# Neighbourhood attention on one core: all products 32 outputs wide, four side by side, and ten key rows for four query rows

## The chip, the cores and the metric

The kernel runs on one core of a Trainium2 chip. The metric is the time of one execution in device microseconds. Times are medians of several runs; the profile comes from one further execution, whose own time is given beside its span.

## The reference, cut to what matters

An image of 224 x 224 pixels with 192 channels goes through one projection to queries, keys and values. Each pixel attends to 49 neighbours: 7 x 7 pixels with a stride of 2 in both directions, shifted inwards at the borders. The weighted values go through a last projection.

```python
qkv = x @ wqkv                      # (1,224,224,192) @ (192,576)
off = jnp.arange(7) * 2
r0 = jnp.clip(jnp.arange(224) - 6, 0, 223 - 12)   # the same for columns
nidx = (r0[:, None] + off)[...] * W + (c0[:, None] + off)[...]
logits = jnp.einsum('bnc,bnkc->bnk', q, k[nidx]) * 192 ** -0.5
out = jnp.einsum('bnk,bnkc->bnc', softmax(logits), v[nidx]) @ wo
```

Because of the stride of 2, pixels of even and odd rows, and of even and odd columns, form four images of 112 x 112 that never mix.

## The kernel before, in words

**Weights folded.** The kernel never makes queries and keys. It computes A = Wq Wk^T (scaled, in `AW`), so that a logit is x_query A x_key, and W = Wv Wo (in `WP`), so that the values are already projected. x lies transposed in SBUF: `XA` and `XB` hold 128 rows each, where `XB` has 64 channels and, in its other 64 rows, marks of rows and columns that push a logit outside the window to about NEG, -1e30. A product over the channels therefore takes two passes (`pas` 0 with `XA`, 1 with `XB`), accumulated in PSUM.

**Steps and pairs.** The work goes in 14 steps n, each with a row class `rc` (even or odd rows) and 16 query rows. A step has 7 pairs of strips (m); a strip s is 16 query rows by 8 query columns, 128 queries, in both column classes `cc`. So there are 98 pairs k. For each, in this order in the code:

- `stage1` (L476): logits of two strips into the PSUM tiles `s` (`SS[0]` and `SS[1]`, 128 x 2 x 256), L501. The stationary operand is `g`, the folded queries; the moving operand is 14 key rows by 14 to 16 columns of `XA` or `XB`. The 128 queries are two halves h of 8 query rows, each with its own 14 key rows (`key_rows`, L468), so a half is a product 64 outputs wide, and the two halves lie in the two 64-column halves of the array, issued in turn. Then DVE reduces to the negative maximum `nmx` (L503).
- `stage1b`: ACT takes the exponentials into `p` (L511), over all 14 key rows.
- `stage2`: 16 transposes of `p` on PE into `pt_ps` (L521), 64 outputs wide, and a copy to `pt_sb` (L523).
- `stage3`: `pt_sb` times the values (`vd`, `vf`) into `o_ps` (L532), 64 wide, with a column of ones that gives the sum.
- `stage4`: DVE divides (L538, L552) and SP and POOL issue the writes (L558, L571).

Between these, for the next step, `w128` and `w64` hold the making of `g` and the values: `g_items` (L405: `pg` in `whole`, `pgh` in `halves`, matmuls at L425 through `both`), copied out by ACT or DVE (L335, L333) and for `pgh` onwards by POOL (L460), and `v_item` (L347: `pv`, matmuls at L345 in `v_mms`). POOL sorts x (L170) and copies `XB` (L160).

**Order.** The code's order of these calls is each engine's order; `in_order` fixes it. Every matmul is one instruction that loads weights (in the profile PEld) and one that streams (PE). All products are 64 outputs wide and come in twos, one for each half of the array.

**NEG in PSUM.** L143 writes NEG once into columns 0 and 1 of each of the 14 rows of 16 in `SS`, which the logits of most strips never write.

Of the kernel before, what the change touches and what calls it, by code (L numbers as in the profile page):

```python
# [21 lines left out]
NSLOT = 14  # L22
NSTEP = 14
NBAND = 14
RP = 48
RW = 2 * S
MM = 16
# [71 lines left out]
def kernel(  # L99
# [40 lines left out]

    SS = [ps_s.tile([128, 2, 256], F32, name=f"s{k}", tag=f"s{k}") for k in range(2)]
    for t in SS:
        nc.vector.memset(_win(t, 0, 128, 0, [[256, 2], [16, 14], [1, 2]]), NEG)  # L143

    def load_items(b):

# [184 lines left out]
    def evac(out_, in_, dve):  # L331
        if dve:
            nc.vector.tensor_copy(out=out_, in_=in_)  # L333
        else:
            nc.scalar.copy(out=out_, in_=in_)  # L335

    def v_mms(pv, at):  # L340
        for cc in range(2):
            for pas in range(2):
                for h in range(2):
                    k = 1 if pas else 2 * cc
                    nc.tensor.matmul(pv[64 * h:64 * h + 64, cc * C:(cc + 1) * C], lhsT=at(k, h), rhs=WP[(cc, pas)][:], start=(pas == 0), stop=(pas == 1))  # L345

    def v_item(rc, cb):  # L347
        def emit(dve):
            pv = ps_g.tile([128, 512], F32, name="pv", tag="pg")
            v_mms(pv, lambda k, h: XS[rc][:, k, cb, 64 * h:64 * h + 64])  # L350
            evac(_win(VF[rc], 0, 128, cb * VP, [[193, 2], [1, C]]), pv[:, 0:2 * C].rearrange("p (t c) -> p t c", c=C), dve)
        return emit

# [8 lines left out]
    def v_first(j):  # L362
        def emit(dve):
            pv = ps_g.tile([128, 512], F32, name="pv", tag="pg")
            v_mms(pv, lambda k, h: _win(XS[1], 0, 128, k * NSLOT * 128 + 128 * j + 64 * h, [[1, 64]]))
            evac(_win(VF[1], 0, 128, (7 + j) * VP, [[193, 2], [1, C]]), pv[:, 0:2 * C].rearrange("p (t c) -> p t c", c=C), dve)
        return emit

# [29 lines left out]
                runs.append([d - d0, 1, mem, pair])  # L398
        return runs

    OUT_A = (0, 64)
    OUT_B = (128, 0)
    GROUPS = ((0, 2), (2, 4), (6, 4), (10, 4))

    def g_items(rc, ti, s0, ns):  # L405
        rows = row_runs(rc, ti)
        w = 8 * ns

        def mm(pg, cc, p0, c0):

            out_ = []
            for (d0, dn, mem, pair) in col_runs(cc, 8 * s0, 8 * s0 + w):
                for (j, n, par, r) in rows:
                    o = _win(pg, p0, 64, j * w + d0, [[w, n], [1, dn]])
                    for pas in range(2):
                        X = (XA, XB)[pas][mem]
                        out_.append((o, AW[(mem, pas)][:, c0:c0 + 64], _win(X, 0, 128, _x(par, r, pair), [[RW, n], [1, dn]]), pas))
            return out_

        def both(a, b):  # L420
            for q in range(max(len(a), len(b))):
                for l_ in (a, b):
                    if q < len(l_):
                        (o, l, r, pas) = l_[q]
                        nc.tensor.matmul(o, lhsT=l, rhs=r, start=(pas == 0), stop=(pas == 1))  # L425

        def put(dst, off, pg, dve, p0=0, pn=128):

            a, m = s0, ns
            if s0 == 0:  # L430
                rr = [_runs8(rc, ti, h) for h in range(2)]
                if len(rr[0]) == len(rr[1]):
                    evac(_win(dst, p0, pn, off, [[64, 2], [8, 8], [1, 8]]), _win(pg, p0, pn, 0, [[8 * w, 2], [1, 8], [w, 8]]), dve)
                else:
                    for h in range(2):
                        for (j0, nj) in rr[h]:
                            evac(_win(dst, p0, pn, off + 64 * h + 8 * j0, [[nj, 8], [1, nj]]), _win(pg, p0, pn, (8 * h + j0) * w, [[1, 8], [w, nj]]), dve)
                a, m = 1, ns - 1
            evac(_win(dst, p0, pn, off + (a - s0) * 128, [[8, 16], [128, m], [1, 8]]), _win(pg, p0, pn, 8 * (a - s0), [[w, 16], [8, m], [1, 8]]), dve)

        def whole(cc):
            def emit(dve):
                pg = ps_g.tile([128, 512], F32, name="pg", tag="pg")
                both(mm(pg, cc, 0, OUT_A[cc]), mm(pg, cc, 64, OUT_A[cc] + 64))
                put(G[rc][cc], s0 * 128, pg, dve)
            return emit

        def halves(dve, direct=False):
            pg = ps_g.tile([128, 512], F32, name="pgh", tag="pg")
            pg1 = ps_o.tile([128, 512], F32, name="pgh", tag="o") if direct else pg  # L450
            both(mm(pg, 0, XDAT[0], OUT_B[0]), mm(pg1, 1, XDAT[1], OUT_B[1]))
            if direct:
                put(G[rc][0], (NSLOT + s0) * 128, pg, False, XDAT[0], 64)
                put(G[rc][1], (NSLOT + s0) * 128, pg1, True, XDAT[1], 64)
                return
            gx = work.tile([128, 512], BF, name="gx", tag="gx", bufs=3)
            put(gx, 0, pg, dve)
            for cc in range(2):
                p = XDAT[cc]
                nc.gpsimd.tensor_copy(out=G[rc][cc][p:p + 64, 1, s0:s0 + ns, :], in_=gx[p:p + 64, 0:ns * 128].rearrange("p (s q) -> p s q", q=128))  # L460

        return [whole(0), whole(1), halves]
# [2 lines left out]
    class Pair:  # L465
        pass

    def key_rows(J, h):  # L468

        i = 2 * J.ti + h  # L470
        if J.rc == 0:
            if i == 0:
                return [(MM - 6, 0, 6), (0, 6, 8)]
            v0 = 8 * i - 6
        else:
            v0 = 8 * i  # L476
        return [(v, v - v0, n) for (v, n) in _wraps(v0, 14)]

    def stage1(J, ab):
        s = 2 * J.m + ab  # L480
        s_ps = SS[ab]


        cols = {0: [(1, 7, S - 7), (8, 8, 0)], 2: [(1, 15, 9)]}.get(s, [(2, 14, 8 * s - 6)])
        lo = cols[0][0]
        for cc in range(2):
            units = []
            for h in range(2):
                u = []
                for (v, k0, n) in key_rows(J, h):  # L490
                    for (q, nq, c) in cols:
                        o = _win(s_ps, 64 * h, 64, cc * 256 + 16 * k0 + q, [[16, n], [1, nq]])
                        for pas in range(2):
                            X = (XA, XB)[pas][cc]
                            u.append((o, G[J.rc][cc][:, pas, s, 64 * h:64 * h + 64], _win(X, 0, 128, _x(J.rc, v, c), [[RW, n], [1, nq]]), pas))
                units.append(u)
            for q in range(max(len(u) for u in units)):
                for u in units:
                    if q < len(u):
                        (o, w, r, pas) = u[q]  # L500
                        nc.tensor.matmul(o, lhsT=w, rhs=r, start=(pas == 0), stop=(pas == 1))  # L501
        nmx = stat.tile([128, 2], F32, name="nmx", tag="nmx")
        nc.vector.tensor_reduce(out=nmx[:], in_=_win(s_ps, 0, 128, lo, [[256, 2], [16, 14], [1, 16 - lo]]), axis=AX.XY, op=ALU.max, negate=True)  # L503
        J.p = PP[J.rc][J.k % 2]
        J.s[ab] = (s_ps, nmx)
# [8 lines left out]
    def stage2(J):  # L514
        pool_ = ps_t if J.k < NP - 1 else ps_g
        pt_ps = pool_.tile([128, 8, 128], BF, name="pt_ps", tag="pt" if J.k < NP - 1 else "pg")
        for ab in range(2):
            for cc in range(2):
                for q in range(2):
                    for h in range(2):  # L520
                        nc.tensor.transpose(pt_ps[64 * h:64 * h + 64, 4 * ab + 2 * cc + q, :], J.p[:, ab, cc, q, 64 * h:64 * h + 64], ident[:])  # L521
        J.pt = work.tile([128, 8, 128], BF, name="pt_sb", tag="pt_sb")
        (nc.scalar.copy if J.n == NSTEP - 1 and J.m < 5 else nc.vector.tensor_copy)(out=J.pt[:], in_=pt_ps[:])  # L523

    def stage3(J, ab):
        rc, s = J.rc, 2 * J.m + ab
        o_ps = (ps_o if J.k < NP - 1 else ps_g).tile([128, 512], F32, name="o_ps", tag="o" if J.k < NP - 1 else "pg")
        V = (VD[rc], VF[rc])
        for cc in range(2):
            for q in range(2):  # L530
                for h in range(2):
                    nc.tensor.matmul(o_ps[64 * h:64 * h + 64, cc * 193:cc * 193 + 193], lhsT=J.pt[:, 4 * ab + 2 * cc + q, 64 * h:64 * h + 64],  # L532
                                     rhs=V[h][:, (s - 1 + q) % NSLOT, cc * C:cc * C + 193], start=(q == 0), stop=(q == 1))
        J.o_ps[ab] = o_ps

    def stage4a(J, ab):
# [73 lines left out]
        v_first(j)(False)  # L610

    t = ps_t.tile([128, 8, 128], BF, name="pt_ps", tag="pt")
    for q in range(16):
        nc.tensor.transpose(t[64 * (q % 2):64 * (q % 2) + 64, q // 2 % 8, :], ident[:, 64 * (q % 2):64 * (q % 2) + 64], ident[:])
    sort1 = sort_items(1, 0, dve)
    for it in xb_items(1, dve) + sort1[2:] + sort1[:2]:
        it()
# [140 lines left out]
```

## Time and profile before

| | |
|---|---|
| time, median of 3 runs (lowest to highest) | 364.49 us (363.73 to 364.56) |
| the profiled execution's own time | 362.85 us |
| its span, first to last instruction | 361.1 us |
| granted TensorE clock, mean | 0.996 |
| matmuls / weight loads on PE | 8,104 / 8,104 |
| matmuls by line: pv L345, g L425, s L501, pt_ps L521, o_ps L532 | 1,624, 1,320, 1,980, 1,568, 1,568 |
| ACT's exponentials L511 | 392 of 450 ns |
| DVE's maxima L503, and scaling L552 | 196 of 564 ns, 179 of 557 ns |
| bytes moved by DMA | 60.79 MB, 168 GB/s over the span |

PE is the matmul side of TensorE and PEld its weight loads, which overlap PE. Busy time is the union of an engine's instructions; matmuls are pipelined, so one of 192 columns is shown with some 250 ns while the next starts long before it ends. "Issue" as a releaser means that an engine was idle and waited for nothing that the profile shows. Queues q1 and so on are DMA queues; a packet is one transfer on one of 16 DMA engines.

### The profile page before, as it was taken

How to read it: one execution, taken by the hardware profiler on the slowest of the kernel's cores; microseconds unless marked ns; L12 is line 12 of the kernel's file. 1: busy time of each engine (PE TensorE's matmuls, PEld its weight loads, DVE VectorE, ACT ScalarE, POOL GpSimd, SP SyncE). 2: the span in 40 equal slices, each digit the busy share in tenths (PEclk: the TensorE clock that was granted, in tenths of full speed). 3: DMA queues.
4: the chain of work that ended last, by engine and by line, in shares of the span. 5: the costliest groups of instructions: out<-in, count | busy, mean ns of one | idle time of the engine just before them, and what ended most of it. 6: DMA issues, size and time to landing. Idle time of an engine off the chain costs nothing.

```text
span 361.1 us, 19455 instructions
## 1 busy us (share of the span) xinstructions
PE 335.6 (93%) x8104; PEld 305.8 (85%) x8104; DVE 313.7 (87%) x743; ACT 307.5 (85%) x821; POOL 285.6 (79%) x456
## 2 busy tenths in 40 slices
PE   3988888998999999999999999999999999999881
PEld 1676777997999899999989999899999999999671
DVE  8967987887998998989989999898998889989992
ACT  3654767997998999989999999999989989999792
POOL 8976799999896986959969699696995878374094
PEclk9999999999999999999999999999999999999998
DMA  9999986697988979899799998988989965634432
GB/s 188 204 175 180 174 172 148 146 199 162 202 177 201 196 164 190 186 194 192 168 183 181 197 190 177 161 213 180 198 178 192 191 146 121 143 97 108 103 80 77
DMA packets 137778, 60.79 MB, mean 168 GB/s; under 512 B 88841, under 2 KB 137166, under 8 KB 137691
## 3 DMA queue, kind: packets, MB, share of 16 engines
q1 hardware_dynamic: 130133, 56.37, 78.3%
q0 software_dynamic: 5520, 1.73, 2.7%
q10 hardware_dynamic: 2038, 1.47, 2.2%
q8 instruction: 63, 1.03, 1.2%
q14 instruction: 24, 0.20, 0.2%
HBM read 0.29 MB, written 19.27 MB: 54 GB/s over the span
## 4 chain that ended last, share of the span: by engine, by line
PE 69%; POOL 10%; DVE 8%; ACT 6%; DMA 3%; issue 2%; SPq 1%; POOLq 0%; DVEq 0%; ACTq 0%
PE pv L345 16%; PE s L501 15%; PE o_ps L532 14%; PE pg L425 10%; PE pt_ps L521 9%; PE pgh L425 5%; POOL out_dram L571 4%; ACT p L511 3%; DVE xb L160 2%; POOL xs L170 2%; POOL out_dram L558 2%; DMA out_dram<-o_sb 1%; DMA vd<-vf 1%; ACT vf L335 1%; DVE nmx L503 1%
## 5 line engine op out<-in xcount | busy, mean ns | idle before, releaser
L511 ACT ACTIVATE p<-s,nmx 128x224 bf16<-128x224 f32 x392 | 149.8, 450 | 24.5 <-DVE nmx L503 22.8
L503 DVE TENSOR_REDUCE nmx<-s 128x2 f32<-128x392 f32 (+1 forms) x196 | 102.4, 564 | 19.9 <-PE s L501 19.4
L552 DVE TENSOR_TENSOR o_sb<-o_ps,rs 128x384 bf16<-128x384 f32 x179 | 99.8, 557 | 7.1 <-DMA out_dram<-o_sb 0.9
L460 POOL COPY g<-gx 64x512 bf16<-64x512 bf16 (+1 forms) x110 | 61.8, 562 | 52.9 <-ACT gx L335 47.1
L345 PE MATMUL pv<-wp,xs 128*64 128x192 bf16 x1624 | 92.7, 250 | 7.1 <-POOL xs L170 1.9
L345 PEld LDWEIGHTS <-xs 128*64 128x64 bf16 x1624 | 78.5, 111 | 20.5 <-issue 8.8
L335 ACT CAST vf<-pv 128x384 bf16<-128x384 f32 x193 | 87.6, 518 | 9.6 <-PE pv L345 5.2
L571 POOL DMA_DIRECT2D out_dram<-o_s x150 | 84.2, 568 | 1.1 <-issue 1.1
L532 PE MATMUL o_ps<-vd,pt_sb 128*64 128x193 bf16 x784 | 82.2, 246 | 2.9 <-ACT pt_sb L523 2.1
L501 PE MATMUL s<-xa,g 128*64 128x196 bf16 (+7 forms) x990 | 82.2, 233 | 1.6 <-issue 0.5
L532 PE MATMUL o_ps<-vf,pt_sb 128*64 128x193 bf16 x784 | 82.1, 246 | 0.0
L501 PE MATMUL s<-xb,g 128*64 128x196 bf16 (+7 forms) x990 | 81.8, 232 | 0.3 <-ACT g L335 0.3
L501 PEld LDWEIGHTS <-g 128*64 128x64 bf16 x1980 | 77.6, 110 | 3.6 <-issue 2.5
L532 PEld LDWEIGHTS <-pt_sb 128*64 128x64 bf16 x1568 | 71.3, 109 | 4.9 <-ACT pt_sb L523 3.2
L523 DVE COPY pt_sb<-pt_ps 128x1024 bf16<-128x1024 bf16 x93 | 63.7, 686 | 5.4 <-PE pt_ps L521 0.6
L521 PE MATMUL pt_ps<-ident,p 128*64 128x128 bf16 x1568 | 63.9, 219 | 0.0
L521 PEld LDWEIGHTS <-p 128*64 128x64 bf16 x1568 | 57.0, 110 | 5.2
L335 ACT CAST g<-pg 128x512 bf16<-128x512 f32 (+4 forms) x136 | 57.6, 471 | 2.0 <-PE pg L425 2.0
L425 PEld LDWEIGHTS <-aw 128*64 128x64 bf16 x1320 | 54.1, 110 | 4.1 <-issue 0.7
L425 PE MATMUL pg<-xb,aw 128*64 128x512 bf16 (+9 forms) x440 | 53.9, 269 | 0.6 <-DVE xb L160 0.6
L425 PE MATMUL pg<-xa,aw 128*64 128x512 bf16 (+9 forms) x440 | 52.0, 270 | 0.0
L170 POOL COPY xs<-xa 128x896 bf16<-128x896 bf16 x50 | 45.1, 928 | 1.4
(75 smaller groups left out, 282.8 us busy)
## 6 DMA issues: line engine op xcount, KB each, us to landing
vd<-vf SPq DMA_DIRECT2D x49, 336.9 KB
out_dram<-o_sb SPq DMA_DIRECT2D x156, 96.0 KB
out_dram<-o_sb SPq DMA_DIRECT2D x26, 78.0 KB
out_dram<-o_s POOLq DMA_DIRECT2D x78, 9.0 KB, 3.9
vd<-vf SPq DMA_DIRECT2D x2, 337.8 KB
vd<-vf ACTq DMA_DIRECT2D x2, 336.9 KB
xa<-in_x_dram SPq DMA_TRANSPOSE x28
out_dram<-o_s POOLq DMA_DIRECT2D x26, 15.0 KB, 3.1
```

The lines of the kernel that those rows point to most:

```text
L335: nc.scalar.copy(out=out_, in_=in_)
L345: nc.tensor.matmul(pv[64 * h:64 * h + 64, cc * C:(cc + 1) * C], lhsT=at(k, h), rhs=WP[(cc, pas)][:], start=(pas == 0), stop=(pas == 1))
L425: nc.tensor.matmul(o, lhsT=l, rhs=r, start=(pas == 0), stop=(pas == 1))
L460: nc.gpsimd.tensor_copy(out=G[rc][cc][p:p + 64, 1, s0:s0 + ns, :], in_=gx[p:p + 64, 0:ns * 128].rearrange("p (s q) -> p s q", q=128))
L501: nc.tensor.matmul(o, lhsT=w, rhs=r, start=(pas == 0), stop=(pas == 1))
L503: nc.vector.tensor_reduce(out=nmx[:], in_=_win(s_ps, 0, 128, lo, [[256, 2], [16, 14], [1, 16 - lo]]), axis=AX.XY, op=ALU.max, negate=True)
L511: nc.scalar.activation(out=J.p[:, ab, cc, :, z:z + 112].rearrange("p q (r k) -> p q r k", k=8), in_=_win(s_ps, 0, 128, cc * 256, [[8, 2], ...
L521: nc.tensor.transpose(pt_ps[64 * h:64 * h + 64, 4 * ab + 2 * cc + q, :], J.p[:, ab, cc, q, 64 * h:64 * h + 64], ident[:])
L523: (nc.scalar.copy if J.n == NSTEP - 1 and J.m < 5 else nc.vector.tensor_copy)(out=J.pt[:], in_=pt_ps[:])
L532: nc.tensor.matmul(o_ps[64 * h:64 * h + 64, cc * 193:cc * 193 + 193], lhsT=J.pt[:, 4 * ab + 2 * cc + q, 64 * h:64 * h + 64], rhs=V[h][:, ( ...
L552: nc.vector.tensor_tensor(out=o_sb[:], in0=_win(o_ps, 0, 128, 0, [[194, 2], [1, C]]), in1=rs[:].unsqueeze(2).to_broadcast([128, 2, C]), op ...
L571: pool_q.append(lambda dst=dst, p=p, m=n * nj, cc=cc: nc.gpsimd.dma_start(out=dst.rearrange("j i c -> i j c"), in_=o_sb[p:p + m, cc, :]))
```

## The change

Every product becomes 32 outputs wide. Four of them, one for each 32-column part of the array, are issued in turn where there were two of 64. That holds for `pv`, `pg`, `pgh`, `s`, `pt_ps`, `o_ps` and the first transposes of the identity. PE's program in the built kernel has 16,168 matmuls and as many weight loads.

For the logits, a part g of the array now holds four query rows. Four query rows see only ten key rows, so `key_rows` gives ten (from row 0 or 4 of the half's fourteen), and the matmul has 10 x 14 columns. The other four key rows of that part keep what stood in PSUM: NEG, which L143 now writes to all 14 x 16 places of both column classes. Strips 0 and 2 of every step, the half with the first eight query rows of the even class and the one with the last eight of the odd class, and the first pair of step 1 still take all fourteen rows. The reduction, the exponentials, the copies and all transfers stay as they are.

```diff
-        nc.vector.memset(_win(t, 0, 128, 0, [[256, 2], [16, 14], [1, 2]]), NEG)
+        nc.vector.memset(_win(t, 0, 128, 0, [[256, 2], [1, 224]]), NEG)
...
+    def side_by_side(ls):
+        for q in range(max(len(l_) for l_ in ls)):
+            for l_ in ls:
+                if q < len(l_):
+                    (o, w, r, pas) = l_[q]
+                    nc.tensor.matmul(o, lhsT=w, rhs=r, start=(pas == 0), stop=(pas == 1))
...
-                for h in range(2):
+                for g in range(4):
                     k = 1 if pas else 2 * cc
-                    nc.tensor.matmul(pv[64 * h:64 * h + 64, cc * C:(cc + 1) * C], lhsT=at(k, h), rhs=WP[(cc, pas)][:], start=(pas == 0), stop=(pas == 1))
+                    nc.tensor.matmul(pv[32 * g:32 * g + 32, cc * C:(cc + 1) * C], lhsT=at(k, g), rhs=WP[(cc, pas)][:], start=(pas == 0), stop=(pas == 1))
...
-                both(mm(pg, cc, 0, OUT_A[cc]), mm(pg, cc, 64, OUT_A[cc] + 64))
+                side_by_side([mm(pg, cc, 32 * g, 64 * cc + 32 * g) for g in range(4)])
...
-            both(mm(pg, 0, XDAT[0], OUT_B[0]), mm(pg1, 1, XDAT[1], OUT_B[1]))
+            side_by_side([mm((pg, pg1)[cc], cc, XDAT[cc] + g, OUT_B[cc] + g) for cc in range(2) for g in (0, 32)])
...
-    def key_rows(J, h):
-        i = 2 * J.ti + h
-        if J.rc == 0:
-            if i == 0:
-                return [(MM - 6, 0, 6), (0, 6, 8)]
-            v0 = 8 * i - 6
-        else:
-            v0 = 8 * i
-        return [(v, v - v0, n) for (v, n) in _wraps(v0, 14)]
+    def key_rows(J, g, full):
+        i, k0 = 2 * J.ti + g // 2, 0 if full else 4 * (g % 2)
+        v0, n = 8 * i - (6 if J.rc == 0 else 0) + k0, 14 if full else 10
+        if v0 < 0:
+            return [(v0 + MM, k0, -v0), (0, k0 - v0, n + v0)]
+        return [(v, k0 + v - v0, m) for (v, m) in _wraps(v0, n)]
...
+                edge = (J.ti, J.rc, g // 2) in ((0, 0, 0), (NSTEP // 2 - 1, 1, 1))
+                for (v, k0, n) in key_rows(J, g, edge or s in (0, 2) or (J.n == 1 and J.m == 0)):
                     for (q, nq, c) in cols:
-                        o = _win(s_ps, 64 * h, 64, cc * 256 + 16 * k0 + q, [[16, n], [1, nq]])
+                        o = _win(s_ps, 32 * g, 32, cc * 256 + 16 * k0 + q, [[16, n], [1, nq]])
...
-                    for h in range(2):
-                        nc.tensor.transpose(pt_ps[64 * h:64 * h + 64, 4 * ab + 2 * cc + q, :], J.p[:, ab, cc, q, 64 * h:64 * h + 64], ident[:])
+                    for g in range(4):
+                        nc.tensor.transpose(pt_ps[32 * g:32 * g + 32, 4 * ab + 2 * cc + q, :], J.p[:, ab, cc, q, 32 * g:32 * g + 32], ident[:])
...
-                for h in range(2):
-                    nc.tensor.matmul(o_ps[64 * h:64 * h + 64, cc * 193:cc * 193 + 193], lhsT=J.pt[:, 4 * ab + 2 * cc + q, 64 * h:64 * h + 64],
-                                     rhs=V[h][:, (s - 1 + q) % NSLOT, cc * C:cc * C + 193], start=(q == 0), stop=(q == 1))
+                for g in range(4):
+                    nc.tensor.matmul(o_ps[32 * g:32 * g + 32, cc * 193:cc * 193 + 193], lhsT=J.pt[:, 4 * ab + 2 * cc + q, 32 * g:32 * g + 32],
+                                     rhs=V[g // 2][:, (s - 1 + q) % NSLOT, cc * C:cc * C + 193], start=(q == 0), stop=(q == 1))
```

More of the change, by code (lines that the diff above doesn't have):

```diff
@@ L349, in emit @@
             pv = ps_g.tile([128, 512], F32, name="pv", tag="pg")
-            v_mms(pv, lambda k, h: XS[rc][:, k, cb, 64 * h:64 * h + 64])
+            v_mms(pv, lambda k, g: XS[rc][:, k, cb, 32 * g:32 * g + 32])
             evac(_win(VF[rc], 0, 128, cb * VP, [[193, 2], [1, C]]), pv[:, 0:2 * C].rearrange("p (t c) -> p t c", c=C), dve)
@@ L364, in emit @@
             pv = ps_g.tile([128, 512], F32, name="pv", tag="pg")
-            v_mms(pv, lambda k, h: _win(XS[1], 0, 128, k * NSLOT * 128 + 128 * j + 64 * h, [[1, 64]]))
+            v_mms(pv, lambda k, g: _win(XS[1], 0, 128, k * NSLOT * 128 + 128 * j + 32 * g, [[1, 32]]))
             evac(_win(VF[1], 0, 128, (7 + j) * VP, [[193, 2], [1, C]]), pv[:, 0:2 * C].rearrange("p (t c) -> p t c", c=C), dve)
@@ L399, in col_runs @@
         return runs
-    OUT_A = (0, 64)
     OUT_B = (128, 0)
@@ L413, in mm @@
                 for (j, n, par, r) in rows:
-                    o = _win(pg, p0, 64, j * w + d0, [[w, n], [1, dn]])
+                    o = _win(pg, p0, 32, j * w + d0, [[w, n], [1, dn]])
                     for pas in range(2):
                         X = (XA, XB)[pas][mem]
-                        out_.append((o, AW[(mem, pas)][:, c0:c0 + 64], _win(X, 0, 128, _x(par, r, pair), [[RW, n], [1, dn]]), pas))
+                        out_.append((o, AW[(mem, pas)][:, c0:c0 + 32], _win(X, 0, 128, _x(par, r, pair), [[RW, n], [1, dn]]), pas))
             return out_
[L420 to L425, printed above, removed]
         def put(dst, off, pg, dve, p0=0, pn=128):
@@ L487, in stage1 @@
             units = []
-            for h in range(2):
+            for g in range(4):
                 u = []
-                for (v, k0, n) in key_rows(J, h):
+                edge = (J.ti, J.rc, g // 2) in ((0, 0, 0), (NSTEP // 2 - 1, 1, 1))
+                for (v, k0, n) in key_rows(J, g, edge or s in (0, 2) or (J.n == 1 and J.m == 0)):
                     for (q, nq, c) in cols:
-                        o = _win(s_ps, 64 * h, 64, cc * 256 + 16 * k0 + q, [[16, n], [1, nq]])
+                        o = _win(s_ps, 32 * g, 32, cc * 256 + 16 * k0 + q, [[16, n], [1, nq]])
                         for pas in range(2):
                             X = (XA, XB)[pas][cc]
-                            u.append((o, G[J.rc][cc][:, pas, s, 64 * h:64 * h + 64], _win(X, 0, 128, _x(J.rc, v, c), [[RW, n], [1, nq]]), pas))
+                            u.append((o, G[J.rc][cc][:, pas, s, 32 * g:32 * g + 32], _win(X, 0, 128, _x(J.rc, v, c), [[RW, n], [1, nq]]), pas))
                 units.append(u)
[L497 to L501, printed above, removed]
+            side_by_side(units)
         nmx = stat.tile([128, 2], F32, name="nmx", tag="nmx")
@@ L530, in stage3 @@
             for q in range(2):
-                for h in range(2):
-                    nc.tensor.matmul(o_ps[64 * h:64 * h + 64, cc * 193:cc * 193 + 193], lhsT=J.pt[:, 4 * ab + 2 * cc + q, 64 * h:64 * h + 64],
-                                     rhs=V[h][:, (s - 1 + q) % NSLOT, cc * C:cc * C + 193], start=(q == 0), stop=(q == 1))
+                for g in range(4):
+                    nc.tensor.matmul(o_ps[32 * g:32 * g + 32, cc * 193:cc * 193 + 193], lhsT=J.pt[:, 4 * ab + 2 * cc + q, 32 * g:32 * g + 32],
+                                     rhs=V[g // 2][:, (s - 1 + q) % NSLOT, cc * C:cc * C + 193], start=(q == 0), stop=(q == 1))
         J.o_ps[ab] = o_ps
@@ L612 @@
     t = ps_t.tile([128, 8, 128], BF, name="pt_ps", tag="pt")
-    for q in range(16):
-        nc.tensor.transpose(t[64 * (q % 2):64 * (q % 2) + 64, q // 2 % 8, :], ident[:, 64 * (q % 2):64 * (q % 2) + 64], ident[:])
+    for q in range(32):
+        nc.tensor.transpose(t[32 * (q % 4):32 * (q % 4) + 32, q // 4, :], ident[:, 32 * (q % 4):32 * (q % 4) + 32], ident[:])
     sort1 = sort_items(1, 0, dve)
```

## The prediction, as made before the change was run

> **What bounds the kernel now.** I read the page first, then stretches of time, the chain of waits in one stretch, and the one idle spot of TensorE that nothing explains. The page's busy line and two of its queue lines:
>
> ```profile
> PE 335.6 (93%) x8104; PEld 305.8 (85%) x8104; DVE 313.7 (87%) x743; ACT 307.5 (85%) x821; POOL 285.6 (79%) x456
> ...
> q1 hardware_dynamic: 130133, 56.37, 78.3%
> ...
> q8 instruction: 63, 1.03, 1.2%
> ```
>
> The reader should see three things. TensorE (PE) has the most work, with DVE and ACT not far below. The DMA engines are busy too. And queue 8 carries instructions: 63 packets of 16 KB. PE's program in the built kernel has 16,240 (8,104 matmuls, as many weight loads, a few of the sequencer's); 1.03 MB over them is 64 B each, so a packet is 256 instructions and queue 8 is PE's. So PE's program is not on the chip: it is fetched while it runs, 256 instructions at a time.
>
> The table by stretches (columns: stretch, PE, PEld, DVE, ACT, POOL busy with counts, granted clock, DMA share, GB/s):
>
> ```profile
> 215.00:240.00 25.00, 24.96 (x587) 23.06 (x583) 23.06 (x57) 23.78 (x64) 21.63 (x32) 1.00 0.99 183
> ...
> 290.00:315.00 25.00, 25.00 (x719) 24.15 (x715) 22.35 (x54) 23.24 (x69) 15.19 (x29) 1.00 0.60 133
> ```
>
> From 90 to 335 us PE has hardly an idle moment, at a granted clock of 1.00; ACT is at 92 to 95% and DVE at 88 to 92%. The chain of waits in one step of that stretch is PE alone:
>
> ```profile
> 187.16 0.66 PE pv L345 x16
> 187.82 0.69 PE s L501 x17
> 188.51 0.67 PE o_ps L532 x16
> 189.18 0.46 PE pgh L425 x4
> 189.64 0.45 PE pt_ps L521 x16
> 190.09 0.46 PE pg L425 x4
> ```
>
> Sixteen matmuls of 192 columns (pv) take 0.66 us, a pair side by side 82 ns; sixteen of 128 (pt_ps) take 0.45, a pair 56. Both are 0.43 ns a column. So PE is bound by the columns that stream through it, two products at a time. That is what the change attacks. But one view speaks of another limit close by, PE's matmuls around 155 us:
>
> ```profile
> 154.94 0.22 PE L501 MATMUL s<-xb,g 128*64 128x120 bf16 x1
> 155.61 0.28 PE L501 MATMUL s<-xa,g 128*64 128x90 bf16 x2 [0.45 <-issue]
> ```
>
> PE stands still from the start at 154.945 to the next at 155.614, released by "issue": by nothing that the profile knows. The matmul that comes late waits for no semaphore and its weights were loaded at 154.947. It is instruction 6,338 of PE's program. In the trace's packet records of queue 8 a packet had started at 153.24, only 2.37 us before PE went on. I then marked the program at instruction 194 and every 256 from there (6,338 is one of the marks). There are 63 marks and 63 packets, and 62 of the packets start between 0.03 us before and 2.43 us after PE reached a mark. The shortest time from a packet's start to the first instruction behind the next mark is 2.37 us at the stall and 2.64 us or more at all the others. The reading I choose: entering one block of 256 instructions asks for the next one, only one is on its way at a time, and a block can be used about 2.37 us after its packet starts. At the stall PE entered the block with nothing queued, and the next packet started at 157.18, 1.56 us later. **One fetch so costs 1.56 + 2.37 = 3.9 us, and PE can't be given more than 256 instructions in that time.** Before, a block lasts 5.2 us on average; the fastest two in a row took 8.1 us together. The limit was just not met.
>
> **The change part by part.**
>
> *Streams.* Counted in the built kernels, the logits (L501) stream 310,464 columns two at a time, 155,232 steps; after it is 482,048 four at a time, 120,512 steps, since most quads take 10 x 14 columns and not 14 x 14. Pairs of 196 start 84 ns apart, 0.43 ns a column: 34,720 steps less are 14.9 us of PE. The other four products (L345, L532, L521, L425) stream what they did, in quads for pairs. What falls short of this: quads of few columns. Pairs of 9 columns start 31 ns apart, so a quad costs 31 ns if four are like two and 62 ns if instructions are passed one by one; there are some 340 of them below 60 columns, so 0 to 11 us. I take 2, near the first case, as each half of the array is seen to run its own load and matmul on its own. Net: 13 us less PE work.
>
> *Instructions.* Matmuls go from 8,104 to 16,168, each with a load: PE's program from 16,240 to about 32,390 instructions, 126 marks for 63. Sequencing itself is cheap: where PE's sequencer stops for a second semaphore (20.587 and 20.760), it passed 22 instructions in the 122 ns between, 5.5 ns each, so 32,390 are 180 us, hidden under the streams. Fetching is not: 256 instructions would hold 2.6 us of streams (PE's 335.6 less 13, over 126 blocks), and a fetch takes 3.9.
>
> *DVE's memset* (L143) grows from 56 to 448 floats a partition, twice: 105 ns each now, at most the 564 ns of the reduction of 392 (L503): 0 to 0.9 us at the start, I take 0.5. Reductions, exponentials, copies, DMAs and their order are unchanged, and POOL's and SP's queues issue the same transfers.
>
> **The sum.** How long is a fetch over the whole run? The request comes when the sequencer, not PE, reaches a mark. Where it stops for a second semaphore its place is known: it was up to 38 instructions ahead of PE, 19 matmuls or 0.8 us. So a fetch takes 0.8 us, the packet's start behind the mark, and 2.37. That start depends on how busy the DMA engines are: 0.0 to 0.7 us in 290 to 335 us (DMA share 0.60 and 0.44), up to 2.3 where the share is 0.8 to 1.0. With 0.5 it is 3.7 us, with 1.5 it is 4.7, with 0.0 it is 3.2. A longer kernel spreads the same bytes to a share of about 0.6, but the start stays loaded; I take 3.9, the stall's own, and keep 3.2 and 4.7. PE reached the first mark at 17.5, the sequencer at 16.7; 125 more marks follow, one per fetch: 125 x 3.9 = 488. Behind the last mark some 200 instructions, 2 us; from the last matmul to the end 8 us, as now (353 to 361.1). 16.7 + 0.5 + 488 + 2 + 8 = 515 us of span. The profiled execution lies 1.75 us above its span (362.85 against 361.1): 517, to be held against that 362.85. The median of the runs, 364.49, is 0.5% above the profiled one, inside the range. **Forecast 517 us**; its own range is 429 (3.2 a fetch) to 616 (4.7). The waits that PE has today vanish under this: ACT, DVE and POOL, at 79 to 87% of 361 us, would sit at 55 to 61%.
>
> [...]
>
> **The rivals.**
>
> A, faster: more than one block is fetched ahead, so that a late packet doesn't matter. It decides from a fetch period of 2.6 us a block downward. For it: only one stall in 63 blocks. Against it: that stall stands at a mark, behind the one packet with the least time before its mark. Then PE falls by 13 us, of which 245/361, 9 us, lie in the stretch from 90 to 335 where PE sets the pace. ACT's idle time there, 1.2 to 2.1 us in 25, is 12 to 20 us in all and leaves room for that. 362.85 - 9 = 354 us (350 to 362).
>
> B, slower, but less: the sequencer passes instructions more slowly over a long time than in that burst. The trace bounds it: 719 matmuls with their loads in the 25 us from 290 are 17.4 ns an instruction, so 5.5 to 17.4. It decides from about 10 ns (323 us of streams / 32,390); at 12 ns it is 389 us and the 29 of the two ends, 418, 1 ns being 32 us. For it: no long stretch is faster than 17.4. Against it: 51 matmuls with their loads in 1 us at 18.52, and the burst.
>
> [...]
>
> C, slower: four products don't run beside each other, only two. Nothing in this trace has four. Then PE's 323 us double to 646, and with the 25 us that PE has idle today the total is about 670.
>
> That the change does not do what it says can be ruled out: the built program has 2,096 matmuls of 10 x 14 and 16,168 in all.
>
> **How the numbers follow.** Fetch-bound: 0.72. A: 0.14. B: 0.08. C: 0.04. Mixtures that end within 0.3% (about what a measurement of this kernel can tell from no change): 0.02. Faster has A's 0.14, same 0.02, slower the other 0.84. The forecast's own range holds perhaps 0.66 of these; to leave out no more than 2 in 10 the range goes down over B and a shorter fetch (2.8 us: 379), where some 0.13 more lie, and stays at 616 above: 375 to 616.
>
> **What would show it.** Right: queue 8 with some 126 packets and 2.07 MB; PE busy below 70%; PE idle put to "issue", over a microsecond, once every 128 matmuls, all through the run, and no clear wait for another engine. ACT, DVE and POOL at 55 to 60%. [...] If stalls stand at the marks but are shorter or longer, the step that failed is the 3.9 us.

## The result, and the profile after

The changed kernel takes 554.55 us (median of 4 runs, 553.98 to 554.95) where the kernel before takes 364.44: a ratio of 1.522, 95% interval 1.520 to 1.525. The forecast was 517 with a range of 375 to 616. The profiled execution has a span of 552.7 us.

The page's busy line, its DMA slices and its queue lines, after:

```profile
PE 362.1 (66%) x16180; PEld 312.2 (56%) x16180; DVE 322.3 (58%) x743; ACT 317.6 (57%) x821; POOL 286.0 (52%) x456
...
DMA  9967558485494764654564656848457424333222
...
q1 hardware_dynamic: 130133, 56.37, 52.5%
...
q8 instruction: 126, 2.06, 1.6%
```

No engine is busy for more than 66% of the span any more. The engines have about the same busy time as before (DVE 322 us against 314, ACT 318 against 307, POOL 286 in both, PE 362 against 336), spread over half as much time again. Queue 8 has twice the packets and twice the bytes: 126 and 2.06 MB.

TensorE's (PE's) waits, longest first (columns: who waited for what, us in total, how often, longest):

```profile
PE s L343 <- issue: 43.9, 29, 2.4
PE o_ps L528 <- issue: 28.3, 20, 2.5
PE pg L343 <- issue: 28.1, 14, 3.0
PE pv L353 <- issue: 26.4, 17, 3.1
PE pt_ps L517 <- issue: 26.0, 21, 2.5
PE pgh L343 <- issue: 4.8, 3, 2.2
PE o_ps L528 <- DVE o_sb L548: 4.1, 3, 2.1
```

Six products, on four lines of the kernel, wait for "issue", 157.5 us in all, and each roughly by its share of the matmuls (`s`: 24% of the matmuls, 28% of this wait; the furthest off is `pg` with 11% and 18%); the most that PE waits for another engine is 4.1. A stop that falls on whichever line happens to be next is a sign of something that the lines don't cause. One such place, PE's matmuls just behind a mark:

```profile
206.80 0.42 PE L353 MATMUL pv<-wp,xs 128*32 128x192 bf16 x10 [1.70 <-issue]
```

Ten matmuls that need nothing but values that have long been there, after 1.70 us of nothing.

With the marks of the prediction (instruction 194 of PE's program and every 256 from there) the trace gives the table below. It is not a view of the profile but a few rows worked out from the start times of PE's instructions and of queue 8's packets, in us:

```
mark  PE there  stopped before it  packet starts behind it  packet to next mark  to the next mark
 40    188.65        2.85                 2.52                     2.52               5.04
 41    193.69        2.50                 1.10                     2.63               3.73
 42    197.42        1.38                 2.19                     2.64               4.83
 43    202.25        2.41                 2.06                     2.49               4.55
 44    206.80        1.95                 1.13                     2.60               3.73
 45    210.53        1.40                 1.15                     2.31               3.45
```

Of some 330 pauses over 150 ns between two starts on PE, 117 stand exactly at the first instruction behind a mark, at no other place of a block more than 5; of the others some 30 belong to the start before 13 us. Behind 20 us there are 116 at marks, together 196.5 us. The first of the 126 marks is reached at 15.4 us, the last at 543.4. That is 4.22 us a block over 125 blocks. With stops at both ends of a block, the packet starts 1.77 us behind the mark (mean of 108), itself takes 1.10, and the next block runs 2.49 us after the packet's start.

Each step of streaming is as fast as forecast. Quads of 192 columns start 82.5 ns apart (pairs before: 82.5), of 140 columns 61.0, of 128 columns 56.0, and of 48 columns 32.0. So four products do run side by side, each quad in the time of a pair.

### The profile page after: what moved, and what is told of

It reads as the page before. It is cut to its first block, busy times and chain, and to the rows that moved or that the text cites. A ratio compares the mean times of both kernels' runs of the same rounds, so it can differ in the third digit from the quotient of the medians.

```text
span 552.7 us, 35609 instructions
## 1 busy us (share of the span) xinstructions
PE 362.1 (66%) x16180; PEld 312.2 (56%) x16180; DVE 322.3 (58%) x743; ACT 317.6 (57%) x821; POOL 286.0 (52%) x456
## 3 DMA queue, kind: packets, MB, share of 16 engines
q8 instruction: 126, 2.06, 1.6%
## 4 chain that ended last, share of the span: by engine, by line
PE 35%; issue 34%; POOL 22%; DVE 5%; ACT 2%; POOLq 0%; ACTq 0%; DVEq 0%
PE o_ps L528 8%; PE pv L353 8%; POOL out_dram L567 7%; PE s L343 7%; PE pg L343 6%; POOL xs L170 5%; PE pt_ps L517 5%; POOL g L460 5%; POOL xb L160 4%; PE pgh L343 3%; POOL out_dram L554 1%; ACT p L507 1%; DVE o_sb L548 1%; DVE xb L160 1%; DVE xs L170 1%
## 5 line engine op out<-in xcount | busy, mean ns | idle before, releaser
L353 PE MATMUL pv<-wp,xs 128*32 128x192 bf16 x3248 | 99.8, 258 | 32.2 <-issue 26.4
L353 PEld LDWEIGHTS <-xs 128*32 128x32 bf16 x3248 | 82.1, 102 | 48.8 <-issue 36.8
L528 PE MATMUL o_ps<-vd,pt_sb 128*32 128x193 bf16 x1568 | 91.5, 254 | 20.7 <-issue 13.9
L343 PEld LDWEIGHTS <-g 128*32 128x32 bf16 x3960 | 72.9, 100 | 54.0 <-issue 48.1
L528 PE MATMUL o_ps<-vf,pt_sb 128*32 128x193 bf16 x1568 | 91.5, 254 | 14.4 <-issue 14.4
L343 PE MATMUL s<-xb,g 128*32 128x140 bf16 (+9 forms) x1980 | 80.0, 224 | 25.9 <-issue 23.8
L528 PEld LDWEIGHTS <-pt_sb 128*32 128x32 bf16 x3136 | 73.0, 99 | 41.8 <-issue 35.5
L343 PE MATMUL s<-xa,g 128*32 128x140 bf16 (+9 forms) x1980 | 80.7, 224 | 22.8 <-issue 20.1
L517 PE MATMUL pt_ps<-ident,p 128*32 128x128 bf16 x3136 | 73.4, 226 | 26.4 <-issue 26.0
L517 PEld LDWEIGHTS <-p 128*32 128x32 bf16 x3136 | 61.9, 100 | 36.7 <-issue 32.3
```

The source lines that it names most:

```text
L353: nc.tensor.matmul(pv[32 * g:32 * g + 32, cc * C:(cc + 1) * C], lhsT=at(k, g), rhs=WP[(cc, pas)][:], start=(pas == 0), stop=(pas == 1))
L517: nc.tensor.transpose(pt_ps[32 * g:32 * g + 32, 4 * ab + 2 * cc + q, :], J.p[:, ab, cc, q, 32 * g:32 * g + 32], ident[:])
L528: nc.tensor.matmul(o_ps[32 * g:32 * g + 32, cc * 193:cc * 193 + 193], lhsT=J.pt[:, 4 * ab + 2 * cc + q, 32 * g:32 * g + 32], rhs=V[g // 2] ...
```

## The experiments

Theory: PE's program comes in blocks of 256 instructions, one fetch at a time, 4.22 us each as in the trace after; a kernel whose blocks hold less work than that waits. Rivals: the width of 32, or four products side by side, costs by itself; the sequencer is slow; the streams still count. "Marks" are blocks entered; "stopped" is the sum of PE's pauses over 0.15 us at the marks, from 20 us on.

| kernel | PE instructions | marks | changes of width | us | stopped at marks, us (times) |
|---|---|---|---|---|---|
| before | 16,240 | 63 | 13 | 364.4 | 2.4 (5; one of them with no semaphore to wait for) |
| mix | 16,128 | 63 | 312 | 379.4 | 0.6 (3) |
| odd32 | 18,088 | 70 | 209 | 377.6 | 4.4 (9) |
| logits32 | 20,200 | 79 | 209 | 391.2 | 20.6 (30) |
| split_some | 25,872 | 101 | 13 | 462.1 | 93.6 (82) |
| others32 | 28,432 | 111 | 210 | 500.7 | 116.5 (100) |
| after | 32,392 | 126 | 14 | 554.6 | 196.5 (116) |
| full14 | 32,392 | 126 | 14 | 559.8 | 188.0 (113) |
| nocopy | 32,379 | 126 | 14 | 527.3 | 180.8 (119) |
| split64 | 32,472 | 127 | 13 | 561.2 | 151.4 (114) |

**split64: the same work in twice the instructions, at the old width.**

```diff
-            for pas in range(2):
-                for h in range(2):
-                    k = 1 if pas else 2 * cc
-                    nc.tensor.matmul(pv[64 * h:64 * h + 64, cc * C:(cc + 1) * C], lhsT=at(k, h), rhs=WP[(cc, pas)][:], start=(pas == 0), stop=(pas == 1))
+            for a in (0, 64, 128):
+                for pas in range(2):
+                    for h in range(2):
+                        k = 1 if pas else 2 * cc
+                        nc.tensor.matmul(pv[64 * h:64 * h + 64, cc * C + a:cc * C + a + 64], lhsT=at(k, h), rhs=WP[(cc, pas)][:, a:a + 64], start=(pas == 0), stop=(pas == 1))
...
-                for (j, n, par, r) in rows:
+                for (j, n, par, r) in halved(rows):
...
-                for (v, k0, n) in key_rows(J, h):
+                for (v, k0, n) in [x for (v, k0, n) in key_rows(J, h) for x in ((v, k0, n // 2), (v + n // 2, k0 + n // 2, n - n // 2))]:
...
+            for (a, b) in ((0, 97), (97, 193)):
...
```

> The kernel before, 64 outputs wide and two side by side, but with most products cut in two or three along the columns that stream (values in three of 64, g, logits and o_ps in two), so that it does the same work in 32,472 instructions of PE, about as many as the changed kernel. Theory (256 instructions per fetch, one fetch at a time, 4.22 us each as in the changed kernel): 127 marks, 126 x 4.22 + 26.5 = 558 us (540 to 575), with PE idle on issue at the marks. Rival (the width of 32 or four products side by side is what costs): only some 2.5 ns more per added pair, about 375 us, no stalls.

Measured: 561.2 us, ratio 1.539 (1.532 to 1.546). This decides the main question. Nothing is 32 wide here, and the kernel is as slow as the changed one. Its chain of waits from 202 to 209 us (start, us, what):

```profile
202.49 0.47 PE pv L346 x30
202.96 1.51 issue
204.47 0.47 PE pv L346 x18
204.95 0.70 PE s L508 x32
205.65 0.70 PE o_ps L540 x32
206.34 0.51 PE pgh L432 x14
206.85 0.45 PE pt_ps L528 x16
207.29 0.47 PE pg L432 x12
207.77 0.71 issue
208.48 0.22 PE pg L432 x2
208.70 0.76 PE pv L346 x48
```

Between the stops the products go at nearly their old pace: the 32 logits of half the size take 0.70 us as the 16 or 17 did 0.69, `o_ps` 0.70 for 0.67. The values, cut in three, are slower where no stop falls among them, 0.76 for 0.66. The rival's 2.5 ns a pair is what the trace of before gives, as an estimate from the starts of PE's instructions: where pairs follow one another without a stop, those of 192 columns start 82.3 ns apart and those of 128 columns 55.7, so 0.416 ns a column and 2.5 ns besides. Here each of the 16 added pairs of the values takes some 6 ns; 4,058 added pairs at that are 24 us of the 197 that this kernel is slower. The stops stand in the middle of a group, at a count of instructions and not at a place in the work.

**split_some: fewer cuts.** The same edit for the values and o_ps alone.

> The kernel before, 64 wide, with only the value products (in three of 64 columns) and o_ps (in two) cut: 25,872 instructions of PE, 101 marks, the same work, and no change of width. Theory: 100 x 4.27 (the mean of the two runs bound by the fetch, 4.22 and 4.30) + 26.5 = 453 us (440 to 465). Rival (time follows streams and a fixed 2.5 ns per added pair): 370 us.

Measured: 462.1 us, ratio 1.269 (1.263 to 1.275), inside the theory's range, far from 370. 82 of the marks stop PE, a block takes 4.39 us on average. The fetch itself is longer here: in the 77 blocks with stops at both ends the packet starts 1.88 us behind the mark and the next block runs 2.54 later, 4.42 in all, under a mean DMA share around the mark of 0.71, where the changed kernel has 0.57.

**others32 and logits32: the change in two parts.**

```diff
# others32, against the changed kernel: memset, key_rows and the logits as before
-            for g in range(4):
+            for h in range(2):
...
# logits32, against the kernel before: memset, key_rows and the logits as in the change
-            for h in range(2):
+            for g in range(4):
```

> The changed kernel with the logits as before (64 wide, fourteen key rows); all other products 32 wide. 28,432 instructions, 111 marks. Theory: 110 x 4.22 + 26.5 = 491 us (475 to 510). Rival (nothing is lost by 32-wide products as such, and no fetch limit): 364 us. Rival (only the ten rows of the logits do harm): 364 us.

> The kernel before with only the logits changed (32 wide, ten key rows); all other products 64 wide. 20,200 instructions, 79 marks. Theory: a block then holds about as much work (4.3 us) as a fetch takes, so blocks dense in logits wait and others do not: some 4.4 us a block, 78 x 4.4 + 26.5 = 370 us (360 to 385). Rival (each 32-wide product costs as in the changed kernel, 190 us over 16,152 of them): 411 us. Rival (no fetch limit, streams shorter): 352 us. [...]

Measured: others32 500.7 us, ratio 1.373 (1.370 to 1.376), as the theory said within its range. logits32's four executions took 380.5, 390.9, 391.5 and 393.5 us (median 391.2): the first lies inside the 360 to 385 expected from the fetch alone, the others above, and all below the 411 of the rival that charges each 32-wide product. Its trace, taken in the execution of 390.9, has two losses, seen here in its chain of waits:

```profile
187.64 0.56 PE s L346 x33
188.21 0.55 issue
188.75 0.46 PE s L346 x11
189.21 0.79 PE o_ps L539 x16
```

The first is a stop in the middle of the logits, where instructions are dense (the trace has thirty stops at marks, 20.6 us). The second is that 16 matmuls of o_ps take 0.79 us and not 0.67, each time behind the 32-wide logits. From 64 to 32 wide two starts lie 176 ns apart (the median), back 154, where two starts in the kernel before lie 42 ns apart on average.

**odd32 and mix: the two losses taken apart.**

```diff
# odd32, against logits32: 32 wide in odd strips only
-            for g in range(4):
+            for g in range(4) if ab else (0, 2):
...
# mix, against logits32: values, transposes and whole g products 128 wide
-                    for h in range(2):
-                        nc.tensor.transpose(pt_ps[64 * h:64 * h + 64, 4 * ab + 2 * cc + q, :], J.p[:, ab, cc, q, 64 * h:64 * h + 64], ident[:])
+                    nc.tensor.transpose(pt_ps[:, 4 * ab + 2 * cc + q, :], J.p[:, ab, cc, q, :], ident[:])
```

> The kernel before with the logits of every second strip (odd s) 32 wide with ten key rows: 18,088 instructions, 70 marks, 5.1 us of work in a block, so hardly a stall; 6.5 us less streams; two changes of width in a step, 196 in all. Theory (the loss of the kernel with all logits 32 wide is about as much from changes of width, 0.13 us each by its trace, as from the fetch): 364.5 - 6.5 + 25 = 383 us (375 to 392). Rival (that loss is the fetch alone): 358 us. Rival (the changes of width alone, the fetch being no limit there): 383 us as well, but then no stall at the marks.

> Logits 32 wide with ten key rows, values, transposes and the full g products 128 wide, o_ps and the half g products 64 wide: 16,128 instructions, 63 marks, as few as before, but some 300 changes of width. Theory: no stall at the marks, 13 us less streams, 298 x 0.13 = 39 us for the changes: 390 us (378 to 402). Rival (only the fetch costs): 351 us, faster than before.

Measured, beside 363.8 for the kernel before: odd32 377.6 us, ratio 1.037 (1.034 to 1.041); mix 379.4, ratio 1.042 (1.039 to 1.046). Both are slower than before though they hardly stop at marks (4.4 and 0.6 us), and both are somewhat faster than I expected. So a change of width costs, and less than 0.13 us: (377.6 - 363.8 + 6.5 - 4.4) / 196 = 0.08 us in odd32, (379.4 - 363.8 + 13 - 0.6) / 299 = 0.09 in mix. That is an estimate: it takes the shorter streams at their full 6.5 and 13 us, and would be lower if they bring less. The chain of mix shows it in the same place, and again at the step from 64 to 128 wide, where 8 full transposes take 0.55 us for the 0.45 that 16 halves took:

```profile
186.93 0.55 PE pt_ps L527 x8
187.48 0.74 PE pg L346 x8
188.22 0.69 PE pv L356 x8
188.91 0.70 PE s L346 x24
189.61 0.79 PE o_ps L538 x16
```

With it the traced execution of logits32 adds up: 364.5 - 13 + 20.6 + 196 x 0.09 = 390 us, for 390.9; why another took 380.5 no trace shows. Why a change of width costs 0.08 to 0.09 us no run shows. So ten key rows do shorten the streams, but neither way of having them is free: in one width the instructions double, in two widths 196 changes cost some 17 us and the streams bring 13. No run was faster than the kernel before; an order of the work with fewer changes was not run.

**full14: is the saving still there underneath?** The changed kernel with fourteen rows everywhere.

```diff
-                for (v, k0, n) in key_rows(J, g, edge or s in (0, 2) or (J.n == 1 and J.m == 0)):
+                for (v, k0, n) in key_rows(J, g, True):
```

> The changed kernel with fourteen key rows for every logit, so without the saving in streams that the change is built on; the number of PE's instructions is the same, 32,392. Theory (PE waits for its instructions, streams lie under the fetch): no difference, 554 us (549 to 560). Rival (streams still set the pace in part): up to 15 us more, 569 us.

Measured: 559.8 us (559.6 to 559.9) against 554.6 (554.0 to 555.0). So it is 5 us longer where the streams are 14.9 us longer. PE stops 8.5 us less at the marks (188.0 for 196.5), so more than half of the longer streams went into time that was lost anyway. The rest is in blocks of 4.27 us and not 4.22. Put side by side, the 111 blocks that end with a stop in both kernels hold 6.4 us of difference, the 14 others -0.9: it is the blocks paced by the fetch that are longer, not the few without a stop. What makes them longer is open.

**nocopy: does the fetch wait for the DMA engines?** The changed kernel with the transfers of vd left out and vf read in their place.

```diff
-        V = (VD[rc], VF[rc])
+        V = (VF[rc], VF[rc])
...
-        eng.dma_start(out=VD[rc][0:64, c0:c1, 0:VP - 1], in_=VF[rc][64:128, c0:c1, 0:VP - 1])
+        pass
```

> The changed kernel without the copies of the values to vd (both halves read vf, so the output is not the reference's): a third of the DMA bytes is left out, PE's instructions stay 32,379. Theory with a fetch that waits for busy DMA engines: the start of a packet behind its mark falls from a mean of 1.77 us towards 1.2, a block from 4.22 to 3.7 us, 125 x 3.7 + 26.5 = 489 us (470 to 520). Rival (a fetch has a fixed time): 554 us.

Measured: 527.3 us, between the two: 27 us less than the changed kernel, where 35 to 85 were expected. Its DMA slices and queue lines:

```profile
DMA  9945245153362531531533726335243211111122
...
q1 hardware_dynamic: 105653, 38.18, 35.8%
...
q8 instruction: 126, 2.06, 1.7%
```

The load is lower on average, but it still comes in bursts. Sorted by the DMA share around the mark (0.5 us before to 1.5 us after it), the packet starts 1.26 us behind the mark below a share of 0.3, 1.55 in between, 1.78 above 0.7; in the changed kernel 1.19, 1.75 and 2.13. The time from the packet to the next mark is 2.5 to 2.6 us at every load in the kernels that stop at most marks. So a block took 3.99 us instead of 4.22, and 125 x 0.23 = 29 us is the difference. A packet starts later where the DMA engines are busier, in the changed kernel 0.9 us later on average at the densest load (2.13 for 1.19), but 1.2 + 2.5 = 3.7 us, an estimate from these means, stay without them. My step from "less DMA" to "3.7 us" took the quiet marks for all marks.

## Why the prediction was right, point by point

- **What bounds the kernel.** Right: streams set the pace before, at 0.43 ns a column, and the limit close behind them was the fetch of instructions. One stop of 0.67 us in the trace of before was its only sign.
- **Streams.** Right: quads of 192, 140 and 128 columns take 82.5, 61 and 56 ns, small ones 32 ns (the lower end, not 62). Under the fetch they are worth little (full14).
- **Instructions.** Right: 126 packets, 2.06 MB, one block at a time, for 32,392 instructions. (The trace has 16,180 matmuls; the 16,168 given ahead of the run is 12 short, the 32,390 is not.) A block of the kernel before lasts 5.4 us from mark to mark, not the 5.2 of the prediction; the sum doesn't use it. The work of a block after the change was to be 2.6 us: 4.22 us less a mean stop of 1.67 is 2.55.
- **DVE's memset.** Two of 432 ns for two of 105: 0.65 us, taken at 0.5. It is without weight.
- **The sum.** The mechanism was right, and one term was too small: the fetch, 3.9 us forecast and 4.22 measured. 125 x 0.32 = 40 us, and the span came out 38 above the 515 forecast (552.7); the ends differ by the other 2 (first mark at 15.4 for 16.7, last part 9.3 for 10). The 3.9 was the one fetch with a clean start in the trace of before, 1.56 + 2.37; 108 such fetches in the trace after have 1.77 + 2.49. It was luck in part that this one fetch lay so near the mean: the starts of the 108 lie between 1.03 and 4.68 us behind their marks. I had expected the load to thin out to a share of 0.6 (it was 0.55 behind 20 us), but fetches wait for the share at their own moment: 43 of the 108 marks stand at over 0.7, where the start takes 2.13.
- **The others.** ACT, DVE and POOL were to sit at 55 to 61% and PE below 70%: 57, 58, 52 and 66%, so POOL a little lower.
- **Rival A**, more than one block ahead: refuted by 117 stops at the marks. In mix and the kernel before, with 5.6 and 5.4 us from mark to mark, hardly anything stops (3 and 5 of 63 marks); in split_some, others32 and the changed kernel, where a block holds less work than a fetch takes, PE stops at 82 of 101, 100 of 111 and 117 of 126 marks.
- **Rival B**, a slow sequencer: refuted. Between stops the changed kernel runs 256 instructions in 2.55 us, 10 ns each, at the pace of its streams.
- **Rival C**, two at a time: refuted by the quads' spacing, 82.5 ns for 192 columns where a pair took the same.

## What to carry to other kernels

Count PE's instructions beside its busy time. In these runs they came 256 to a block with one fetch in flight, 4.22 us a block in the changed kernel and an estimated 3.7 with quiet DMA engines (1.2 + 2.5), so some 14 to 16 ns for an instruction of PE, loads of weights included. A kernel of small matmuls that packs the array better can run into this while each of its products streams as forecast, as this one did; a lone stop on "issue" with no wait, where a block of 256 instructions begins, was the sign of it before the change (0.67 us from start to start). Changing the width of products back and forth cost an estimated 0.08 to 0.09 us each time in odd32 and mix, which is worth only what the next few matmuls gain by it.

## What the runs showed of the hardware that was not expected

- **The time of a block comes in steps.** From one mark to the next the changed kernel mostly takes 3.45, 3.73, 4.00, 4.28, 4.55, 4.83 or 5.10 us, steps of 0.274 apart: of the 108 blocks with stops at both ends, 99 lie within a quarter of such a step. What makes the steps was not tested.
- **One half of the array ran ahead of the other.** In the kernel before at 20.37 us a matmul of one half started 9 ns before one of the other half that is earlier in program order. So at that place the program's order was not kept between the halves.
- **The granted clock was lower behind stretches with long stops.** It is 0.953 on average in the changed kernel for 0.996 before. The trace after has it at one half in 14 stretches of 3.4 us and at the very end. In the 3.4 us ahead of each of the 14 PE is busy for 41% at most, ahead of all other such stretches for 40% or more, and inside them quads of 192 columns start 160 ns apart for 82. Two stretches in a row (columns: stretch, its length, PE busy with the count of matmuls, granted clock, DMA share, GB/s):

```profile
91.10:94.50 3.40, 1.31 (x76) 0.99 0.71 164
94.50:97.90 3.40, 3.40 (x80) 0.50 0.49 100
```

  In full14 and split64 the line between the two kinds is less sharp. nocopy has as many stops, but shorter ones (1.52 us on average for 1.69), 7 such stretches and 0.973. What they cost in time was not tested.
